# A new order for the 1215 steps of a Mamba-2 and SwiGLU kernel

## The chip, the cores and the metric

The kernel runs on one core of a Trainium2 chip. The metric is the device time of one execution in microseconds (us). Before the change the median of three runs is 358.98 us (358.59 to 359.54). One further execution was taken by the profiler; all rows come from it.

## The reference

```python
def _attn_ref(x, a, B, C):              # x (4, 8, 768, 32), a (4, 8, 768), B and C (4, 8, 768, 16)
    log_a = np.log(np.clip(a, 1e-06, 1.0))
    for c in range(nc):                 # chunks of 32
...
        L = np.exp(cum[:, :, :, None] - cum[:, :, None, :]) * causal
        y_intra = np.einsum('bhij,bhjd->bhid', np.einsum('bhin,bhjn->bhij', Cc, Bc) * L, xc)
        y_inter = np.einsum('bhin,bhnd->bhid', Cc, state) * np.exp(cum)[:, :, :, None]
        y[:, :, sl] = y_intra + y_inter
        state = decay_full[:, :, None, None] * state + np.sum(Bx, axis=2)

def _moe_ref(x, w_gate, w_val, w_out, rms_g):   # x (3072, 256), d_ff 1536
    xn = x / np.sqrt(np.mean(x * x, axis=-1, keepdims=True) + 1e-06) * rms_g
    g = xn @ w_gate
    return (g * (1.0 / (1.0 + np.exp(-g))) * (xn @ w_val)) @ w_out
```

All inputs and the output are fp32. The output y of the first part, with its heads side by side, is the x of the second.

## The kernel before

The 3072 tokens are cut into 12 pairs (256 tokens, p = 0 to 11) for the first part and into 6 blocks (512 tokens, blk = 0 to 5) for the second. The 1536 hidden units are cut into 12 slices of 128 (f = 0 to 11), and the weights are fetched in 18 pieces (k = 0 to 17).

Most products of the second part run in three matmuls of a shorter format (fp32r) in place of one in fp32: an operand is cut into a high part, a low part and a third part, and the three partial products are added in PSUM. For the weights these parts are made on the chip from the fetched bits: `pow` (two ACT operations of L272, `e<-wr,kinks` and `e<-e,kinks`), `mana` (ACT, L306) or `man` (DVE), `wt` (DVE), and then `wH` (ACT, L341), `wHv`, `wL`, `wM`, `wMp`.

The work is written as 1215 steps in one string, `order` (line 1422 on). Each step is a name with numbers, and stands for a function that issues instructions on one engine, or a few. A loop goes through the string and calls them one after the other. Every engine executes its instructions in that order, and buffers are handed out in that order too: six rings, among them the eight banks of PSUM. A step that needs a bank waits until the step that last reads that bank has run. So the string decides what waits for what. Nothing reorders it later.

The steps that the following speaks of:

- `X.blk.f.m` (`gv_split`, L1173): the gate (m = 0) or the value (m = 1) of one slice for one block: six fp32r matmuls with 512 columns. `F` (L1163) and `early` (L1126) are the fp32 forms that the first block uses for a few slices.
- `silu.blk.f` (ACT, L272, `hx<-gv`) and `hid.blk.f` (DVE) turn gate and value into a hidden slice. `hH`, `hL`, `hK` cut it into three parts.
- `OX`, `OY`, `OF` (L1242, L1220, L1248): the product of a hidden slice with the output weights.
- `A.p` (L843), `S.p`, `yi.p` (L929, `y<-T,S`) and `ya.p` (L929, `y<-L,x`): the state sums, the states, and the two parts of y. These matmuls use small tiles of the array: 64x32 for A and ya, 32x64 for yi and for `gb` (L778). `ms` (L1020 and L1027) sums squares, with tiles of 128x32 from block 1 on.
- `yt.blk.k` (ACT, L1005 and L1008): copies two banks of y out of PSUM. `sq` (ACT) squares y, `rs` takes the roots for the norm, `xH`, `xL`, `xK` cut the normed x into its three parts.
- `sums` (L622 and L629), `row`, `turn` (L704), `T`, `Tt`, `L`, `exp`: decays and turned operands of the first part. `i:y.0` and `i:y.1` are the y products of the first two pairs, before early.0.0, the first product of the second part.
- `put`, `puta`, `putva`: the output is copied out of PSUM and stored.

ACT has one set of functions loaded at a time. Exp and silu are in different sets, and where the order of the steps goes from one to the other, a table load (L264 for the silu set, L266 for the exp set) is issued by a helper. A number behind a star in the string (`i:c*2`) asks for that many filler matmuls (L131), whose result is not used, ahead of that step's own.

Of the kernel before, what the change touches and what calls it, by code (L numbers as in the profile page):

```python
# [50 lines left out]
def kernel(  # L51
# [15 lines left out]
    NB, NH, S, D = x.shape  # L67
# [5 lines left out]
    T = NB * S  # L73
# [181 lines left out]
    parts = {}  # L255
# [130 lines left out]
    mid = mids[:, 0]  # L386
# [958 lines left out]
    def token_out():  # L1345
# [77 lines left out]
        i:warm i:a i:set i:bc.0 i:ident i:bc.1 i:bc2.1.1 i:ones i:zeros i:ident16 i:whole i:kinks  # L1423
        i:idle.7 i:after i:never i:fetch.2 i:whole16 i:mean i:part i:head i:part2 i:sel i:after2
        i:mask.0.0 i:upto i:mid i:upto2 i:eps i:aT i:la0 i:log i:mask.0.1 i:mids i:log4.0.4 i:hmask
        p:x.1 i:c*2 p:x.0 i:r.0 i:cx p:turn.0 i:d i:tmask i:gcol i:log4.4.2 i:dx i:log4.6.2
        i:fetch.0 i:parts.0 i:middles p:turn.1 p:Tt.1.0 i:sums.0.1 i:Tb.0 i:mask.1.1 i:cc p:T.0
        i:sums.1.1 i:exp.0.1 i:fetch.6 i:g.0.1 i:exp.1.1 i:sums.0.0 p:scale.1 p:Tt.1.1 i:last.1
        p:scale.0 p:T.1 i:r.1 i:g.0.0 i:exp.0.0 i:L.0.1 i:tok i:Tl.1 i:g.1.1 i:pow.2 i:mask.1.0
        i:parts.1 i:L.0.0 i:last.0 i:sums.1.0 i:A.1 i:exp.1.0 i:row.1 i:A.0 i:L.1.1 i:g.1.0 i:Tl.0  # L1430
        p:S.0 i:tokout p:bc.2 i:pow.0 i:fetch.1 i:y.0 i:rowe.1 p:bc.3 i:sq.0 i:row.0 i:limit i:L.1.0
        i:sums.3 p:S.1 i:man.0 i:pow.6 i:y.1 i:wt.0 i:rowout.1 i:yt.0 p:dT.2 i:fetch.4 p:turn.2
        i:sq.1 i:yt.1 i:early.0.0 i:open i:man.6 i:wt.6 i:man.1 i:fetch.5 i:man.2 i:exp.3 b:ms.0
        i:rowe.0 i:cav.3 i:early.0.1 i:pow.1 i:sums.2 i:wHv.6 i:wt.1 b:rs.0 i:wt.2 i:fetch.3 p:x.2
        p:dT.3 p:x.3 i:fetch.12 i:fetch.8 p:T.2 i:xn i:exp.2 p:Tt.2.1 p:turn.3 p:Td.2 i:early.1.0
        i:norm.0 p:Tt.2.0 p:T.3 p:Tt.3.1 i:wHv.2 i:rowout.0 i:man.4 i:early.1.1 b:F.0.2.0 i:pow.4
        p:scale.3 i:wt.4 p:Tt.3.0 i:norm.1 b:xH.0.1 i:pow.5 i:ca.2 b:gb.1 i:wL.6 b:L.1.1 b:F.0.4.0
        i:fetch.10 p:scalep.2 b:xH.0.0 b:silu.0.2 i:silu.0 b:xLp.0.1 i:pow.3 b:L.1.3 p:Td.3
        b:F.0.3.0 b:L.1.2 b:L.1.0 b:xK.0.1 b:xK.0.0 i:wHv.1 i:mana.3 b:xLp.0.0 p:A.2 p:S.2 p:A.3
        i:wt.3 b:silu.0.4 i:man.5 i:pow.12 b:F.0.5.0 i:wMp.6 b:X.0.7.0 b:X.0.6.0 i:wHv.3 p:S.3  # L1440
        p:qb.5 b:silu.0.5 i:wL.3 b:silu.0.3 i:fetch.9 i:pow.8 i:man.12 i:fetch.11 p:yi.2 i:wt.5
        p:ya.2 i:pow.10 b:silu.0.6 i:wM.3 p:yi.3 p:ya.3 i:fetch.13 i:wHv.5 b:sq.1.0 i:hid.0 i:wt.12
        p:qc.5 i:wL.5 b:X.0.2.1 i:silu.1 b:yt.1.1 i:mana.10 b:hid.0.2 i:gains i:mana.8 p:vB.5
        i:wMp.5 b:silu.0.7 i:wt.10 b:sq.1.1 b:X.0.3.1 i:fetch.7 i:wt.8 i:pow.13 i:man.13 b:yt.1.0
        b:sqav.1 p:spread.8 i:fetch.14 i:hid.1 i:fetch.17 i:pow.11 b:OF.0.0.1 b:X.0.5.1 b:X.0.4.1
        b:ms.1 p:spread.10 b:OF.0.1.1 i:wHv.10 b:OF.0.0.0 i:wt.13 i:wL.10 i:man.11 b:OF.0.2.0
        i:wMp.10 b:rs.1 i:wH.4 i:wH.8 p:qc.4 b:rb.1 b:hid.0.3 b:hid.0.5 i:wt.11 b:OF.0.2.1 i:man.7
        i:wHv.11 i:pow.9 i:man.9 i:wL.11 i:wL.1 p:dT.5 b:OF.0.3.1 i:mana.14 b:X.0.11.0 p:vC.5
        i:pow.7 b:OF.0.1.0 i:wMp.11 p:scale.5 b:hid.0.4 p:spread.11 i:fetch.15 i:wt.9 b:X.0.10.0
        i:man.17 b:OF.0.3.0 i:wL.8 i:wH.9 i:pow.17 i:wL.9 b:silu.0.11 b:X.0.11.1 b:X.0.10.1  # L1450
        b:silu.0.10 i:wM.8 i:wM.9 p:sub.10 p:qb.4 i:wt.17 i:wt.7 i:wH.7 b:X.0.9.1 b:X.0.9.0 p:subp.8
        i:pow.14 p:x.4 i:wH.0 p:vC.4 b:X.0.8.0 b:hid.0.10 p:Tt.5.1 p:spread.9 p:dT.4 p:Tt.5.0
        b:silu.0.8 i:wL.7 b:X.0.8.1 b:OF.0.10.0 i:wM.1 i:wM.7 b:xn.1.1 i:wL.4 p:Tt.4.1 b:X.0.7.1
        b:OF.0.10.1 p:subp.11 b:X.0.6.1 i:wt.14 i:fetch.16 b:OF.0.4.1 i:mana.15 p:scalep.4 b:xn.1.0
        b:hid.0.7 b:OF.0.5.1 b:xH.1.1 b:xK.1.1 b:silu.0.9 p:A.4 p:x.5 p:ex.10 b:xLp.1.1 p:vB.4
        b:xH.1.0 p:ex.8 p:subp.9 b:hid.0.9 p:Tt.4.0 i:pow.15 p:ex.11 b:xL.1.0 b:xK.1.0 p:ex.9
        b:OF.0.4.0 b:X.1.10.0 p:qc.6 p:S.4 i:wH.17 b:hid.0.8 b:X.1.10.1 b:silu.1.10 p:ca.9 p:qc.7
        i:wMp.4 b:hid.0.6 b:X.1.11.0 b:hid.0.11 p:cav.8 p:qb.7 p:A.5 b:hid.1.10 b:X.1.6.0 b:OF.0.5.0
        b:silu.1.11 b:hH.0.7 b:silu.1.6 b:X.1.8.0 b:X.1.8.1 p:Tdp.4 p:scale.6 p:S.5 b:silu.1.8
        i:wL.0 p:ca.11 p:ca.10 i:wt.15 b:hL.0.7 i:wL.17 i:wM.0 b:gb.2 b:hid.1.8 p:vC.7 b:X.1.7.0  # L1460
        i:wH.14 b:L.2.0 b:X.1.11.1 b:silu.1.7 i:mana.16 i:wMp.17 b:L.2.1 p:scalep.7 b:L.2.2 i:wH.15
        b:X.1.0.0 b:L.2.3 i:pow.16 p:Tdp.5 p:vC.6 b:table.2 p:yi.4 i:wL.15 b:silu.1.0 i:wt.16
        i:wM.15 p:x.6 b:hHv.0.11 i:wH.13 p:ya.4 i:wH.16 p:yi.5 p:Tt.7.0 b:hid.1.11 p:ya.5 b:sq.2.0
# [12 lines left out]
        b:OX.1.11.1 b:OX.1.8.1 b:put.0.0 b:hL.1.0 b:OX.1.6.0 b:OX.1.11.0 b:L.3.1 b:xH.2.1 i:wL.13
        b:OX.1.0.1 b:OX.1.6.1 b:L.3.2 b:xLp.2.1 b:xK.2.1 b:L.3.0 b:hH.1.7 p:qc.8 b:L.3.3 b:hHv.1.5
        b:OX.1.0.0 p:Td.7 b:OX.1.8.0 p:qc.11 b:hL.1.7 b:hK.1.7 b:xH.2.0 b:hH.1.1 p:yi.6 p:ya.6
        b:xL.2.0 p:scalep.8 b:xK.2.0 p:yi.7 i:wL.14 p:ya.7 b:hid.1.2 i:wMp.14 p:spread.19 b:OX.1.7.1
        p:vC.8 b:exps.5 p:spread.18 b:yt.3.1 b:sq.3.1 p:qb.10 b:hHv.1.2 b:OX.1.7.0 b:X.2.0.0 p:vB.8  # L1480
        b:X.2.10.0 b:X.2.2.0 b:hHv.1.4 b:hL.1.5 p:spread.16 b:X.2.4.0 b:yt.3.0 p:qc.9 b:hK.1.4
        b:silu.2.10 b:hLp.1.4 b:hK.1.2 p:subp.19 b:hK.1.5 b:hK.1.1 b:X.2.10.1 i:wMp.13 b:silu.2.0
        b:OX.1.4.1 b:OX.1.4.0 b:sq.3.0 p:scale.11 b:X.2.0.1 p:ex.19 b:X.2.7.0 b:hL.1.2 b:silu.2.7
        b:hid.2.0 b:hL.1.1 p:spread.17 b:X.2.9.0 b:OX.1.2.1 b:OX.1.2.0 b:hHv.1.10 b:X.2.11.0 p:vB.10
        p:x.8 b:hLp.1.10 b:hK.1.10 b:OX.1.1.0 b:hH.1.3 p:vC.11 b:OX.1.5.0 p:vB.11 b:silu.2.11
        p:sub.18 b:silu.2.2 p:vC.9 b:sqa.3 b:hHv.1.9 p:Tt.8.0 p:A.8 b:ms.3 p:ca.19 p:sub.16 p:qc.10
        p:S.8 b:OX.1.1.1 p:Tt.8.1 p:sub.17 b:X.2.2.1 b:hL.1.9 b:hLp.1.3 b:OX.1.10.0 b:rs.3
# [101 lines left out]
```

## Time and profile before

| | |
|---|---|
| median of the runs | 358.98 us |
| profiled execution, span | 357.0 us |
| matmuls on PE, in the program | 2394 |
| table loads on ACT | 34 |
| DMA packets, MB | 94556, 27.88 |

The engines in the profile are PE (TensorE matmuls), PEld (its weight loads), DVE (VectorE), ACT (ScalarE), POOL (GpSimd) and SP (which issues DMAs). A timeline row has its start in us, its duration in us, the engine, the line, the operation, output and inputs, the tile of the array, shape and type, and how many like records are put together. An fp32 matmul leaves two records. Matmuls are pipelined, and the ends of their records reach into the next; times of PE are therefore read from start to start. The rows of a stretch give, for each engine, busy us and the number of its instructions, then the granted clock, the share of the DMA engines and GB/s.

### The profile page before, as it was taken

The numbers are of one execution on the slowest core, as the hardware profiler recorded it, in microseconds if no ns is written. First come the engines' busy times: TensorE is split into PE (matmuls) and PEld (weight loads), VectorE is DVE, ScalarE is ACT, GpSimd is POOL, SyncE is SP. The second block draws the span as 40 slices with busy tenths as digits, with TensorE's granted clock in tenths as the row PEclk, the third lists the DMA queues.
The fourth block names the chain that finished last, engine by engine and source line by source line (L and its number), as shares of the span: only waits on it lengthen the run. The fifth ranks groups of instructions, "written<-read, shape, count | busy, mean of one in ns | idle before, by whom it ended". The sixth has DMA issues, their size and how long they took to land.

```text
span 357.0 us, 8314 instructions
## 1 busy us (share of the span) xinstructions
PE 352.7 (99%) x3329; PEld 285.0 (80%) x3329; DVE 283.5 (79%) x507; ACT 196.6 (55%) x338; POOL 91.1 (26%) x91
## 2 busy tenths in 40 slices
PE   8999999999999999999999999999999999999996
PEld 5677578887888878878788788788788888888896
DVE  6899999999998999987887955877357582875791
ACT  3888999994756757494154672463345342112510
POOL 4125314256211326540123320025101111311000
PEclk9999999999999999999999999999999999999999
DMA  8978986672261345443123011200010021001003
GB/s 105 213 124 242 281 233 189 176 162 51 42 155 55 96 81 136 80 76 75 31 64 102 8 31 29 48 14 2 7 31 0 1 37 23 0 0 31 0 2 88
DMA packets 94556, 27.88 MB, mean 78 GB/s; under 512 B 77463, under 2 KB 92471, under 8 KB 94519
## 3 DMA queue, kind: packets, MB, share of 16 engines
q1 hardware_dynamic: 92438, 27.23, 33.4%
q8 instruction: 26, 0.43, 0.5%
q10 hardware_dynamic: 2080, 0.13, 0.4%
q14 instruction: 12, 0.09, 0.1%
HBM read 23.68 MB, written 3.67 MB: 77 GB/s over the span
## 4 chain that ended last, share of the span: by engine, by line
PE 98%; DVE 1%; issue 0%
PE gv L1173 53%; PE o L1242 19%; PE o L1248 8%; PE y L929 3%; PE o L1220 2%; PE gv L1163 2%; PE gv L1126 2%; PE g L778 2%; PE A L843 1%; PE g L771 1%; PE e L608 1%; PE y L904 1%; PE e L622 1%; PE ms L1027 0%; PE idle L447 0%; PE row L1311 0%
## 5 line engine op out<-in xcount | busy, mean ns | idle before, releaser
L1173 PE MATMUL gv<-xh,wh 128*128 128x512 f32 x272 | 87.0, 401 | 0.0
L272 ACT ACTIVATE hx<-gv 128x512 f32<-128x512 f32 x70 | 40.2, 595 | 80.2 <-PE gv L1173 36.7
L1173 PE MATMUL gv<-xl,wp 128*128 128x512 f32 x272 | 84.1, 390 | 0.0
L1173 PE MATMUL gv<-xk,wp 128*128 128x512 f32 x272 | 83.8, 390 | 0.0
L1096 DVE SCALAR_TENSOR_TENSOR hk<-hx,hh 128x512 fp32r<-128x512 f32 x65 | 53.0, 827 | 25.4 <-PE o L1242 18.9
L1094 POOL TENSOR_TENSOR hl<-hx,hh 128x512 fp32r<-128x512 f32 x21 | 29.7, 1418 | 131.1 <-DVE hk L1096 30.4
L1173 PEld LDWEIGHTS gv<-xl,wp 128*128 128x128 f32 x272 | 51.1, 188 | 11.0
L1173 PEld LDWEIGHTS gv<-xk,wp 128*128 128x128 f32 x272 | 51.1, 188 | 10.9
L1173 PEld LDWEIGHTS gv<-xh,wh 128*128 128x128 f32 x272 | 50.0, 188 | 10.8 <-issue 0.6
L1188 DVE SCALAR_TENSOR_TENSOR hx<-gv,hx 128x512 f32<-128x512 f32 x70 | 47.0, 684 | 13.4 <-PE gv L1173 12.4
L341 ACT ACTIVATE hh<-hx 128x512 fp32r<-128x512 f32 x37 | 22.8, 629 | 39.8 <-PE o L1242 11.9
L1242 PE MATMUL o<-hh,wh 128*128 128x512 f32 x96 | 37.9, 395 | 0.0
L1242 PE MATMUL o<-hl,wp 128*128 128x512 f32 x96 | 37.4, 390 | 0.0
L1242 PE MATMUL o<-hk,wp 128*128 128x512 f32 x96 | 37.4, 390 | 0.0
L1094 DVE TENSOR_TENSOR hl<-hx,hh 128x512 fp32r<-128x512 f32 x44 | 31.1, 721 | 2.8 <-PE o L1242 1.3
L266 ACT ACT_TABLE_LOAD x17 | 21.8, 1283 | 1.1 <-PEq L1573 0.8
L264 ACT ACT_TABLE_LOAD x17 | 21.8, 1283 | 0.3
L1242 PEld LDWEIGHTS o<-hh,wh 128*128 128x128 f32 x96 | 18.0, 188 | 4.2 <-issue 0.4
L336 POOL TENSOR_TENSOR wp<-wh,wp 128x512 fp32r<-128x512 f32 x9 | 13.0, 1449 | 32.6 <-DVE wp L328 25.0
L1242 PEld LDWEIGHTS o<-hk,wp 128*128 128x128 f32 x96 | 18.0, 188 | 3.8
L1242 PEld LDWEIGHTS o<-hl,wp 128*128 128x128 f32 x96 | 18.0, 188 | 3.6
L328 DVE SCALAR_TENSOR_TENSOR wp<-wh,w 128x512 fp32r<-128x512 f32 x27 | 19.6, 751 | 0.0
(184 smaller groups left out, 548.2 us busy)
## 6 DMA issues: line engine op xcount, KB each, us to landing
L<-rowd SPq DMA_DIRECT2D x32, 128.0 KB
x<-in_x_dram SPq DMA_DIRECT2D x24, 128.0 KB
wr<-in_moe_w_out_dram SPq DMA_DIRECT2D x6, 511.5 KB
wr<-in_moe_w_gate_dram SPq DMA_DIRECT2D x5, 511.5 KB
wr<-in_moe_w_val_dram SPq DMA_DIRECT2D x5, 511.5 KB
out_dram<-ob SPq DMA_DIRECT2D x28, 64.0 KB
bc<-in_B_dram SPq DMA_DIRECT2D x23, 64.0 KB
bc<-in_C_dram SPq DMA_DIRECT2D x23, 64.0 KB
```

The source lines that it names most:

```text
L264: nc.scalar.preload_act_table(AF.Silu)
L266: nc.scalar.preload_act_table_set("natural_log_exp_and_others")
L272: nc.scalar.activation(**operands)
L328: nc.vector.scalar_tensor_tensor(out=(low_parts, mixed_parts)[i][k], in0=high_parts[k], scalar=(-UP, GAIN)[i], in1=view(ws[k], shape), op0 ...
L336: nc.gpsimd.tensor_tensor(out=mixed_parts[k], in0=high_parts[k], in1=low_parts[k], op=ALU.subtract)
L341: nc.scalar.activation(out=out, in_=in_, func=AF.Copy, scale=scale)
L1094: engine.tensor_tensor(out=out, in0=v, in1=high, op=ALU.subtract)
L1096: nc.vector.scalar_tensor_tensor(out=out, in0=v, scalar=REST, in1=high, op0=ALU.mult, op1=ALU.subtract)
L1173: nc.tensor.matmul(out=o, lhsT=weights_of(m, t, f)[part], rhs=view(x, [P, TB], F32R), start=(part == t == 0), stop=(part == 2 and t == 1))
L1188: nc.vector.scalar_tensor_tensor(out=v, in0=o, scalar=gain(blk, f), in1=v, op0=ALU.mult, op1=ALU.mult)
L1242: nc.tensor.matmul(out=o, lhsT=w[:, b * P:(b + 1) * P], rhs=v, start=opens, stop=True, skip_group_check=True)
L1248: nc.tensor.matmul(out=o[:, j * DM:(j + 1) * DM], lhsT=v[:, tk], rhs=w, start=opens, stop=True, skip_group_check=True)
```

## The change

The string is replaced by another order of the same 1215 steps. The multiset of the steps is the same but for one: `i:c*2` becomes `i:c`, so the two filler matmuls are gone (2392 matmuls in the program). The number of operations of all other kinds stays, except for the table loads, which the order of exp and silu decides: 38 in place of 34. Nothing else changes; the lines behind the string move by six.

```diff
@@ -1420,134 +1420,140 @@
     order = """
...
-        p:x.1 i:c*2 p:x.0 i:r.0 i:cx p:turn.0 i:d i:tmask i:gcol i:log4.4.2 i:dx i:log4.6.2
...
+        i:r.0 i:log i:c i:upto2 i:fetch.0 i:middles i:sel p:x.1 p:turn.0 i:tmask i:cx i:gcol
...
```

Three places show what moves. The first is PE at the y products of block 1, pairs 2 and 3. `y<-T,S` is yi, `y<-L,x` is ya, `gv` is an X step, `o<-w,hx` an OF step; xN counts like instructions in a row. Before:

```order
L1173 MATMUL gv<-xk,wp 128x512 x2
L929 MATMUL y<-T,S 64x64 x16
L929 MATMUL y<-L,x 32x64 x32
L929 MATMUL y<-T,S 64x64 x12
L929 MATMUL y<-L,x 32x64 x32
L1173 MATMUL gv<-xh,wh_822 128x512 x2
```

And now:

```order
L1173 MATMUL gv<-xk,wp 128x512 x2
L929 MATMUL y<-L,x 32x64 x64
L929 MATMUL y<-T,S 64x64 x28
L1248 MATMUL o<-w,hx 128x256 x8
L1027 MATMUL ms<-sq,mean 32x128 x4
L1173 MATMUL gv<-xh,wh_891 128x512 x2
```

The two yi and the two ya stand together, which leaves one change of tile between them in place of three; four OF steps and the sums of squares of block 1 follow at once. The y products of the other blocks are put together in the same way.

The second place is ACT from the squares of block 1 to the second copy of its y. `sq<-y` is sq, `hx<-gv` and `u<-u` silu, `w<-wr,kinks` mana, `wh` wH, the pairs of `e<-` pow, and the two rows of `yt<-y` are yt.1.1 and then yt.1.0. Before:

```order
L272 ACTIVATE sq<-y 128x4x64 x2
L272 ACTIVATE u<-u 128x512
L1005 COPY yt<-y 128x4x64
L1008 COPY yt<-y 64x4x64 x2
L306 ACTIVATE w<-wr,kinks 128x512 x2
L272 ACTIVATE hx<-gv 128x512
L272 ACTIVATE sq<-y 128x4x64 x2
L272 ACTIVATE e<-wr,kinks 128x512
L272 ACTIVATE e<-e,kinks 128x512
L1005 COPY yt<-y 128x4x64
L1008 COPY yt<-y 64x4x64 x2
```

And now:

```order
L272 ACTIVATE sq<-y 128x4x64 x4
L306 ACTIVATE w<-wr,kinks 128x512
L1005 COPY yt<-y 128x4x64
L1008 COPY yt<-y 64x4x64 x2
L341 ACTIVATE wh_999<-w 128x512
L272 ACTIVATE hx<-gv 128x512
L272 ACTIVATE e<-wr,kinks 128x512
L272 ACTIVATE e<-e,kinks 128x512
L272 ACTIVATE e<-wr,kinks 128x512
L272 ACTIVATE e<-e,kinks 128x512
L341 ACTIVATE wh_1041<-w 128x512
L1005 COPY yt<-y 128x4x64
```

Between the two copies now stand two pow and two wH in place of two mana, the squares and one pow. On PE, three X steps (X.0.3.1, X.0.8.0, X.0.9.0) follow the sums of squares, and X.0.2.1 behind them is given the bank that the second copy empties.

The third place is ACT around the first hidden slices of block 1. `L<-L` is the exponential of the decays (`ex`), `hx<-gv` silu. Before:

```order
L266 ACT_TABLE_LOAD
L272 ACTIVATE L<-L 128x512
L341 ACTIVATE xh<-yt 128x512
L272 ACTIVATE L<-L 128x512
L341 ACTIVATE T<-T,tmask 128x256
L272 ACTIVATE e<-wr,kinks 128x512
L272 ACTIVATE e<-e,kinks 128x512
L272 ACTIVATE L<-L 128x512 x2
L341 ACTIVATE wh_1343<-w 128x512
L264 ACT_TABLE_LOAD
L272 ACTIVATE hx<-gv 128x512 x2
```

And now, with silu.1.11 between two of the exponentials and silu.1.10 first behind them:

```order
L272 ACTIVATE L<-L 128x512
L264 ACT_TABLE_LOAD
L272 ACTIVATE hx<-gv 128x512
L266 ACT_TABLE_LOAD
L272 ACTIVATE L<-L 128x512 x2
L341 ACTIVATE T<-T,tmask 128x256
L264 ACT_TABLE_LOAD
L272 ACTIVATE hx<-gv 128x512 x4
```

One silu has moved in among the exponentials, and each side of it has a table load.

More of the change, by code (lines that the diff above doesn't have):

```diff
@@ L1428 @@
[L1428 to L1463, printed above, removed]
```

224 lines of the change are left out of this document (133 added, 91 removed).

## The prediction

> **What bounds the kernel now.** I read the page's busy shares and its chain first, then the wait view, then the stretches of the span, then the timelines of TensorE (PE) and ScalarE (ACT).
>
> ```profile
> span 357.0 us, 8314 instructions
> PE 352.7 (99%) x3329; PEld 285.0 (80%) x3329; DVE 283.5 (79%) x507; ACT 196.6 (55%) x338; POOL 91.1 (26%) x91
> PE 98%; DVE 1%; issue 0%
> PE idle L447 <- DVE warm L489: 1.1, 1, 1.1
> ```
>
> The span is 357.0 us, PE is busy for 99% of it, the chain that ends last is PE for 98%, and the wait view (last row) knows one wait of PE in the whole run: 1.1 us at the start. So only three things can move the time: how long PE's own stream takes, a wait that is new in it, or the stretch before its first matmul and behind its last. The last matmul starts at 353.64 and the span ends 3.4 us later, with the copy and the store of the last output:
>
> ```profile
> 353.64 0.28 PE L1220 MATMUL o<-wp,hk 128*128 128x256 f32 x1
> ```
>
> How near the others are to making PE wait differs by stage:
>
> ```profile
> core 0: us, PE busy (x) PEld busy (x) DVE busy (x) ACT busy (x) POOL busy (x), PEclk, DMA share, GB/s
> 41.00:72.00 31.00, 31.00 (x316) 25.16 (x315) 30.82 (x59) 29.52 (x53) 8.01 (x6) 1.00 0.75 205
> 126.00:357.00 231.00, 227.92 (x1866) 188.96 (x1853) 165.03 (x262) 99.61 (x163) 48.79 (x39) 1.00 0.18 38
> ```
>
> Between 41 and 72 us ACT is busy 29.5 of 31.0 us and VectorE (DVE) 30.8. Nobody has slack there; a step that comes some us earlier in PE's order than its operand in ACT's becomes a wait. Behind 126 us ACT is busy for 99.6 of 231 us and DVE for 165.0, so the new order is free there to put PE's work as it likes. The granted clock is 1.00 throughout.
>
> **What PE's stream gains.** The multiset of steps is the same, so almost every matmul keeps its duration. What an order can change is how often PE goes from one shape of tile to another. Pair products as they stand now, two A products alone and side by side, and one row of weight loads:
>
> ```profile
> 93.59 0.49 PE L929 MATMUL y<-T,S 32*64 32x64 f32 x32
> 94.00 0.86 PE L929 MATMUL y<-L,x 64*32 64x64 f32 x64
> 94.79 0.49 PE L929 MATMUL y<-T,S 32*64 32x64 f32 x32
> ...
> 77.01 0.45 PE L843 MATMUL A<-x,Bd 64*32 64x64 f32 x32
> 77.39 0.48 PE L1248 MATMUL o<-w,hx 128*128 128x256 f32 x1
> ...
> 107.67 0.86 PE L843 MATMUL A<-x,Bd 64*32 64x64 f32 x64
> 108.45 0.74 PE L1173 MATMUL gv<-xh,wh 128*128 128x512 f32 x2
> ...
> 94.00 0.70 PEld L929 LDWEIGHTS y<-L,x 64*32 64x32 f32 x64
> ```
>
> From start to start, yi takes 0.41 us and ya 0.79. The order now makes yi, ya, yi, ya of two pairs; the change makes yi, yi, ya, ya (or ya, ya, yi, yi): two changes between small shapes fewer for each of five blocks. With the sums, A and g products counted too, I find 20 changes between small shapes before and 9 after: 11 fewer. Their price isn't in any row by itself. Low end: a stretch of 64 records of one shape (two A, 107.67 to 108.45) takes 0.78, no less than twice the stretch of 32 (77.01 to 77.39: 0.38, so 0.76); merging then brings 0. High end: in such a stretch 64 weight loads take 0.70 of 0.79 us, so 0.09 is left over at a change, and about 0.14 if the next operands load meanwhile. I take 0.09: 11 x 0.09 = **1.0 us** gained, between 0 and 1.5. One small stretch fewer between large products (15 instead of 16) saves a change in and a change out, at 0.09 to 0.14 each some 0.25. Together **1.3 us**. The two filler matmuls (L131) that go belong to the head.
>
> **The head, up to the first split product.** Until 22.8 us the end is set by a chain over PE, ACT and DVE, after it by PE alone.
>
> ```profile
> 23.28 1.89 PE L1126 MATMUL gv<-yt,w 128*128 128x256 f32 x8
> ...
> 27.68 0.44 PE L622 MATMUL e<-row,sel 32*64 32x64 bf16 x32
> ...
> 28.27 0.66 PE L704 MATMUL tp<-ident,bc 128*128 128x128 f32 x4
> ...
> 40.94 1.03 PE L1173 MATMUL gv<-xh,wh 128*128 128x512 f32 x2
> 41.81 0.62 PE L1173 MATMUL gv<-xl,wp 128*128 128x512 f32 x2
> 42.27 0.62 PE L1173 MATMUL gv<-xk,wp 128*128 128x512 f32 x2
> ...
> 53.56 2.64 PE L1248 MATMUL o<-w,hx 128*128 128x256 f32 x11
> ```
>
> The first output products come about 1.3 us earlier in the new order, but sums.2 (27.68 to 28.27: 0.59), sums.3, the two row sums and turn.2 are put between them and early.0.0, which so starts near 23.6 instead of 23.28. Since sums.2 is no longer behind it, that is a gain of 0.2 at most. Then F.0.5.0 waits for weight piece 4 at about 32.4, as late as it comes now. I take the first X at 41.0 as in 40.94: **0**, +-0.5. Two weights of PE's first microseconds:
>
> ```profile
> 2.76 1.01 PE L608 MATMUL e<-whole,ident 128*128 128x512 bf16 x2
> 9.30 0.60 PE L608 MATMUL e<-whole,ident 128*128 128x512 bf16 x2
> ```
>
> The same mask products take 1.01 at 2.76 us and 0.60 at 9.30. By the Trainium skill ("TensorE: Matmul & The Clock Gate", Part 1) PE runs at half rate until it has been busy for about 3.4 us, so taking fillers away speaks against the change; by that rule the four early masks could cost up to 0.8 us more, but the granted clock in the rows here reads 1.00 and these products wait for nothing in the chain that ends at 22.8, so the sum stays.
>
> **The wait that ACT adds.** In the new order, X.0.2.1 takes the bank that the first copy of yt.1.0 empties, and ACT has much ahead of that copy. The durations, from start to start:
>
> ```profile
> 26.07 0.69 ACT L272 ACTIVATE r<-ms,eps 128x512 f32<-128x512 f32 x1
> ...
> 33.13 0.62 ACT L341 ACTIVATE xh<-xn 128x512 fp32r<-128x512 f32 x1
> 33.65 0.77 ACT L272 ACTIVATE e<-wr,kinks 128x512 f32<-128x512 int16 x1
> 34.45 0.72 ACT L272 ACTIVATE e<-e,kinks 128x512 int16<-128x512 f32 x1
> 35.08 0.61 ACT L341 ACTIVATE xh<-xn 128x512 fp32r<-128x512 f32 x1
> 35.71 1.28 ACT L264 ACT_TABLE_LOAD   x1
> 37.00 0.60 ACT L272 ACTIVATE hx<-gv 128x512 f32<-128x512 f32 x1
> ...
> 47.58 0.37 ACT L1005 COPY yt<-y 128x256 f32<-128x256 f32 x1
> ...
> 48.74 1.43 ACT L306 ACTIVATE w<-wr,kinks 128x512 f32<-128x512 uint32 x2
> 50.06 0.60 ACT L272 ACTIVATE hx<-gv 128x512 f32<-128x512 f32 x1
> 50.53 0.66 ACT L272 ACTIVATE sq<-y 128x256 f32<-128x256 f32 x2
> 51.06 0.78 ACT L272 ACTIVATE e<-wr,kinks 128x512 f32<-128x512 int16 x1
> ...
> 52.51 0.36 ACT L1005 COPY yt<-y 128x256 f32<-128x256 f32 x1
> ```
>
> From rs.0 to the copy the new order has: rs.0 1.25 (two operations like the 0.69 at 26.07); eight pow at 1.43 (33.65 to 35.08), 11.4; six high parts at 0.53, 3.2; four turned tiles and one row of decays at about 0.4 (the like of the copy at 47.58: 0.37 of 128x256), 2.1; one table load 1.29; eight silu at 0.5, 4.0; three mana at 0.66, 2.0; two sq at 0.53, 1.1; yt.1.1 1.16. Sum 27.5, and some 0.5 of waits in between. The same sum over the order of before gives 26.6; measured is 52.51 - 26.07 = 26.44. rs.0 comes 0.5 later in the new order (the early steps are behind sums.2): 26.6 + 27.5 + 0.5 = 54.6, with the copy's 0.36 it is 55.0. PE is there earlier: from 41.0 five X of three pairs at 0.46 (41.81 to 42.27), 6.9, with 0.4 lost behind F (40.94 to 41.81 is 0.87), the y products of two pairs 2.2, four OF at 0.86 (2.64 for 11 of three steps' 12 records), 3.4, ms 0.4 and the changes around them 0.3, is 54.6. So PE waits **0.4 us**, between 0 and 2. Behind the waiting X.0.2.1 stands all the rest of PE's work, so it counts in full. The second place is ACT between 71 and 88 us:
>
> ```profile
> 72.94 1.28 ACT L266 ACT_TABLE_LOAD   x1
> ...
> 79.29 1.28 ACT L264 ACT_TABLE_LOAD   x1
> ```
>
> Here are two loads; the new order has four (38 in all instead of 34), 2 x 1.28 = 2.6 us more for ACT, and X.1.6.1 needs the bank of silu.1.10. Counted on from the copy by the same durations, ACT ends that at about 86.2 and PE is there at 88.4: 2.2 us to spare, so 0. By the Trainium skill ("ScalarE: Activation LUTs", What ACT_TABLE_LOAD costs) a switch costs a drain of 1.38 us beside the load's 1.28; by that rule four loads would take 5.5 us more and PE would wait 3.3 there, which makes 361.5. The trace has no room for it: the load at 35.71 starts when the operation before it ends (35.08 + 0.61), and the next one starts 1.29 later. Behind 126 us no step of the new order stands nearer to its operand than DVE's and ACT's lead allows, but for the last hK, which reaches OX.5.11.0 some 0.1 ahead; the last steps (OY products, one copy by ACT, one by DVE) are the same two kinds, so the 3.4 us behind the last matmul stay.
>
> **Sum.** 357.0 + 0 - 1.3 + 0.4 = 356.1 for the span. The median of the runs is 358.98, the span 357.0, so 2.0 lie around it; the profiled execution is taken as a median one. **358.2 us** (0.8 below 358.98). About 0.3%, or 1.08 us, is what a measurement can tell from no change: faster means below 357.9, slower above 360.06.
>
> **The rivals.**
> *The wait doesn't come.* If ACT is at the copy 0.5 sooner (as in 26.07 for rs.0), 0.4 of wait falls away, and if a change between shapes is worth its high end, 0.5 more is gained: 358.2 - 0.9 = 357.3, with bounds of 356.5 (a head 0.5 to 0.8 shorter too) and 357.8 (the wait alone). For it: ACT's rows leave ends 0.06 to 0.1 inside the next, so its pace is as good as I took it. Against it: the eight pow ahead of yt.1.0.
> *Merging brings nothing.* The A rows (0.78 for twice 0.38) are the nearest, and by them 1.0 of gain falls away: 359.2, no change.
> *ACT becomes the bound between 41 and 88 us.* With whole durations instead of start to start (pow 0.06 and silu 0.1 longer) eight of each make X.0.2.1 wait 1.3 more. ACT then slips on at the same rate over the next 31 us, 1.4 more, and with 0.6 for the waits of the two further loads it goes past the 2.2 us to spare at X.1.6.1; from there each 0.1 of slip is a 0.1 of PE. A slip of 3.3 costs 1.1 there: 358.2 + 1.3 + 1.1 = 360.6, slower. For it: ACT's 29.5 of 31.0 us. Against it: it holds today with the same operations.
> *The reordering doesn't reach the engines* isn't open: each executes its part of the list in order.
>
> **How the numbers follow.** Forecast 358.2, own range 357.4 to 359.0: 0.42 (faster 0.13, same 0.29). No wait: 0.28 (faster 0.26, same 0.02). Merging brings nothing: 0.12 (same 0.10, slower 0.02). ACT the bound: 0.18 (slower 0.16, same 0.02). Faster 0.39, same 0.43, slower 0.18. The range, 356.6 to 360.7, leaves out the lower end of the first rival and what ACT could lose beyond its price.
>
> **What would show it.** In the profile of the changed kernel: the first X near 41.0; a wait of PE for yt's copy (L1005) of about 0.4 us near 54.6 and none at silu near 88; y products as two stretches a block with one change, together 2.2 instead of 2.4; ACT loads x19 and x19; the last matmul near 352.7 with 3.4 behind it. The prediction is wrong if PE shows waits of over 1 us anywhere, or if the merged y stretches take as long as the four of before.

## The result, and the profile after

The changed kernel takes 372.63 us (median of 4 runs, 371.34 to 373.53) against 358.83 before (median of 4): 1.0376 times as long, with a 95% interval of 1.0351 to 1.0401. That is 13.8 us slower, far outside the range that was given.

From the page of the changed kernel, its busy shares, table loads and the chain that ended last:

```profile
span 371.8 us, 8293 instructions
...
PE 355.8 (96%) x3327; PEld 285.0 (77%) x3327; DVE 286.9 (77%) x507; ACT 202.7 (55%) x342; POOL 93.8 (25%) x91
...
PE 63%; DVE 21%; SPq 8%; issue 5%; DMA 3%; ACT 0%; POOL 0%; DVEq 0%
...
L266 ACT ACT_TABLE_LOAD x19 | 24.4, 1283 | 2.2 <-issue 1.9
L264 ACT ACT_TABLE_LOAD x19 | 24.4, 1283 | 0.3
```

PE, which carried 98% of the chain, now carries 63%, and DVE 21%. PE's idle time is 371.8 - 355.8 = 16.0 us, where it was 4.3: 11.7 of the 14.8 us that the span has grown. The other 3.1 is more busy time of PE. A part of it stands right behind the waits: a row of eight `early` records takes 1.99 us behind the wait of 1.4 us, and 1.89 without a wait.

Whom PE waits for, in the wait view of the changed kernel (us in total, times, longest; `...` stands for rows left out, among them the 1.4 us at the start):

```profile
PE g L778 <- DVE T L193: 1.5, 1, 1.5
PE gv L1126 <- DVE w L312: 1.4, 1, 1.4
...
PE gv L1173 <- DVE xk L1096: 1.3, 2, 1.0
PE gv L1163 <- DVE w L312: 1.3, 1, 1.3
PE y L929 <- DVE L L801: 1.1, 3, 0.6
PE gv L1173 <- DVE wp L328: 1.0, 1, 1.0
PE o L1242 <- POOL hl L1094: 0.9, 1, 0.9
...
PE gv L1173 <- ACT hx L272: 0.2, 1, 0.2
```

Nearly every row has DVE's name, in many different steps. ACT, which the prediction followed, is there once, with 0.2 us. The waits begin at early.1.0, the third of the `early` products, and end by 146 us, but for the 0.9 us for POOL, which come at 255.7. In the stretch from 22.8 to 110 us DVE is as busy as before (85.60 us of 87.20, against 85.45), but it gets through less: 143 operations in place of 160. The first row is of the kernel before, the second of the changed one; behind the stretch and its length come PE, PEld and then DVE, each with its busy time and its count:

```profile
22.80:110.00 87.20, 87.20 (x1067) 67.96 (x1064) 85.45 (x160) 72.46 (x131) 32.46 (x29) 1.00 0.65 162
```

```profile
22.80:110.00 87.20, 78.42 (x911) 58.92 (x910) 85.60 (x143) 66.83 (x113) 35.49 (x29) 1.00 0.62 152
```

So DVE's single operations have become slower. Where it begins can be seen in DVE's timeline of the changed kernel, with POOL's for the same time behind it:

```profile
24.02 0.73 DVE L312 SCALAR_TENSOR_TENSOR w<-w,e 128x512 int16<-128x512 int16 x1
...
26.67 1.36 DVE L300 TENSOR_SCALAR w<-wr 128x512 f32<-128x512 uint32 x1
...
28.15 1.46 DVE L312 SCALAR_TENSOR_TENSOR w<-w,e 128x512 int16<-128x512 int16 x1
...
31.99 0.68 DVE L1139 TENSOR_TENSOR u<-gv,r 128x512 f32<-128x512 f32 x1
32.59 0.67 DVE L1139 TENSOR_TENSOR hx<-gv,r 128x512 f32<-128x512 f32 x1
33.19 0.41 DVE L300 TENSOR_SCALAR w<-wr 128x512 f32<-128x512 uint32 x1
33.71 1.63 DVE L312 SCALAR_TENSOR_TENSOR w<-w,e 128x512 int16<-128x512 int16 x1
```

```profile
25.57 3.46 POOL L644 TENSOR_SCALAR_AFFINE_SELECT L<-L 64x1024 f32<-64x1024 f32 x2 [0.25 <-ACT L L272]
...
31.88 2.86 POOL L1094 TENSOR_TENSOR xl<-xn,xh 128x512 fp32r<-128x512 f32 x2 [1.82 <-ACT xh L341]
```

The same operation (L312, `wt`) takes 0.73 us at 24.02, started with POOL idle, and 1.46 and 1.63 while POOL runs; `man` (L300) takes 0.41 or 1.36. The two long `wt` end 0.58 and 0.61 us after the POOL operation that they met, the long `man` 0.28: each 0.12 to 0.15 us less than it takes alone. So they wait for POOL's operation to end, and then do their work. This holds over the whole of both traces: the stretched operations with two 128x512 fp32 operands, 0.65 to 0.68 us alone, end 0.54 to 0.55 us after POOL's, whether they lose 0.2 us or 1.1, and those that take 0.41 alone end 0.27 to 0.29 after it. One `man`, at 33.19, takes its 0.41 although POOL runs: it started within 0.02 us of POOL's operation. The two L1139 rows run beside POOL without losing anything; they read PSUM (`gv`). In the order of before, the same mask on POOL stands elsewhere (POOL's timeline of the kernel before):

```profile
29.54 2.64 POOL L644 TENSOR_SCALAR_AFFINE_SELECT L<-L 64x1024 f32<-64x1024 f32 x2 [5.12 <-ACT L L272]
```

There DVE had begun xn (L1070) before it, and then ran L747 and L1139, which read PSUM. Only one operation, the following `wHv` of 1.04 us, was held up.

Over both traces, these are the DVE operations that find a POOL operation running when they start, with at least 0.2 us of it to come (from 20 us on). The first number of each pair is how many of them are stretched, which means over 0.15 us longer than the shortest tenth of the same line and shape in the two traces:

```
                                          before           after
one operand or the result in PSUM         0 of 39          0 of 26
transposes L193, SBUF to SBUF, one input  0 of 8           0 of 3
all others, operands in SBUF only         42 of 46         44 of 46
```

The Trainium skill ("SBUF — State Buffer", Who interferes with whom) says that VectorE's second pair of SBUF ports is GpSimd's only pair, and that an operation of VectorE with two SBUF inputs (against one of GpSimd that reads SBUF), or in a mode that uses both ports, and one of GpSimd exclude one another for their whole length, while one with a single SBUF input outside such a mode does not contend. The first two rows of the table agree with that, and the third does where there are two inputs; `man` and `wHv`, which have a single SBUF input and are held up too, agree if they run in such a mode, which no record shows. It is the rule that bore on this change, and my prediction didn't use it.

In all, these operations lose 27 us before and 31 after, and what matters is where. Between 22.8 and 110 us, where DVE is busy 98% of the time, the operations of before lose 7.0 us, 12 of them over 0.25 us each; those of the changed order lose 15.7 us, 23 of them over 0.25 us. Where the experiments below speak of the stretch "up to 110 us", this sum is meant.

### The profile page after: what moved, and what is told of

It is laid out like the page before. It is cut to its first block, busy times and chain, and to the rows that moved or that the text cites. A ratio compares the mean times of both kernels' runs of the same rounds, so it can differ in the third digit from the quotient of the medians.

```text
span 371.8 us, 8293 instructions
## 1 busy us (share of the span) xinstructions
PE 355.8 (96%) x3327; PEld 285.0 (77%) x3327; DVE 286.9 (77%) x507; ACT 202.7 (55%) x342; POOL 93.8 (25%) x91
## 4 chain that ended last, share of the span: by engine, by line
PE 63%; DVE 21%; SPq 8%; issue 5%; DMA 3%; ACT 0%; POOL 0%; DVEq 0%
PE gv L1173 37%; PE o L1242 16%; PE o L1248 3%; SPq L160 3%; DVE wp L328 2%; PE o L1220 2%; DVE hx L1188 2%; DVE w L312 2%; DVE w L300 2%; PE gv L1163 2%; DVE hk L1096 1%; DVE L L801 1%; DVE S L872 1%; SPq L173 1%; PE g L778 1%
## 5 line engine op out<-in xcount | busy, mean ns | idle before, releaser
L1173 PE MATMUL gv<-xh,wh 128*128 128x512 f32 x272 | 85.6, 396 | 1.2 <-DVE hk L1096 0.7
L1094 POOL TENSOR_TENSOR hl<-hx,hh 128x512 fp32r<-128x512 f32 x21 | 30.8, 1475 | 127.3 <-PE o L1242 52.4
L1096 DVE SCALAR_TENSOR_TENSOR hk<-hx,hh 128x512 fp32r<-128x512 f32 x65 | 51.2, 800 | 14.2 <-PE o L1242 12.0
L341 ACT ACTIVATE hh<-hx 128x512 fp32r<-128x512 f32 x37 | 22.7, 627 | 35.2 <-PE o L1242 9.7
L1094 DVE TENSOR_TENSOR hl<-hx,hh 128x512 fp32r<-128x512 f32 x44 | 33.5, 768 | 9.8 <-PE o L1242 5.1
L336 POOL TENSOR_TENSOR wp<-wh,wp 128x512 fp32r<-128x512 f32 x9 | 14.2, 1584 | 37.8 <-DMA wr<-in_moe_w_val_dram 20.2
L644 POOL TENSOR_SCALAR_AFFINE_SELECT L<-L 64x512 f32<-64x512 f32 (+1 forms) x18 | 16.0, 887 | 21.2 <-DMA r<-roots 9.9
```

The costliest lines, as they stand in the source:

```text
L336: nc.gpsimd.tensor_tensor(out=mixed_parts[k], in0=high_parts[k], in1=low_parts[k], op=ALU.subtract)
L341: nc.scalar.activation(out=out, in_=in_, func=AF.Copy, scale=scale)
L644: nc.gpsimd.affine_select(out=L[r], in_=L[r], pattern=[[0, L.shape[1]], [1, HC]], compare_op=ALU.is_ge, fill=0.0, base=0, channel_multipli ...
L1094: engine.tensor_tensor(out=out, in0=v, in1=high, op=ALU.subtract)
L1096: nc.vector.scalar_tensor_tensor(out=out, in0=v, scalar=REST, in1=high, op0=ALU.mult, op1=ALU.subtract)
L1173: nc.tensor.matmul(out=o, lhsT=weights_of(m, t, f)[part], rhs=view(x, [P, TB], F32R), start=(part == t == 0), stop=(part == 2 and t == 1))
```

## The experiments

Two theories stood against one another. *Collision*: the new order puts DVE's SBUF-only operations on top of POOL's, and DVE, which has no slack up to 110 us, comes too late for PE. *List*: DVE's new list has work ahead of urgent steps, whatever POOL does. A third was added later: *late results*, PE and DVE wait for what POOL makes. In the labels, a is the changed kernel, b the one before. A kernel that leaves work out gives another result; only its time is used.

### One mask on POOL left out (a_no_ca2)

```diff
-        p:turn.3 i:ca.2 i:wL.6 p:T.3
+        p:turn.3 i:wL.6 p:T.3
```

> The changed kernel without one step: the causal mask of pair 2 on POOL (ca.2, 3.4 us on POOL from 25.57 on) is left out and nothing takes its place. Theory 1, collision (a DVE operation that touches only SBUF and finds POOL running waits until POOL's operation ends): man.1 (1.36 us) and wt.1 (1.46 us) go back to 0.41 and 0.73, early.1.0 no longer waits for wt.1 (1.44 us in the changed kernel), and the first split product comes 1.4 to 2.9 us earlier than 43.95; the time falls by 1 to 2.9 us. Theory 2, list (DVE simply has too much work ahead of the urgent steps, whatever POOL does): DVE's list is the same, so the wait and the time stay within 0.5 us.

Measured: 371.47 us (369.93 to 372.53). The median is 1.2 below the changed kernel's, within what collision gave, though the ranges of the runs overlap by a little. The clock hides a part: PE's granted clock was 0.994 and 0.995 over three of the four runs (at half speed from 106.4 to 109.9 us in the profiled one) and 1.00 in the fourth, which took 369.93 us, 2.7 less than the changed kernel, whose runs were all at 1.00. DVE's timeline is clearer than the time:

```profile
26.91 0.41 DVE L300 TENSOR_SCALAR w<-wr 128x512 f32<-128x512 uint32 x1
...
27.44 0.73 DVE L312 SCALAR_TENSOR_TENSOR w<-w,e 128x512 int16<-128x512 int16 x1
...
32.24 1.63 DVE L312 SCALAR_TENSOR_TENSOR w<-w,e 128x512 int16<-128x512 int16 x1
```

Both operations are back at 0.41 and 0.73, and PE's first wait for `wt` fell from 1.4 to 0.2 us. The first split product starts at 42.47 instead of 43.95. The next `wt` (32.24) still runs into a POOL operation (xLp) and PE's second wait, 1.3 us, stays.

### Eight POOL steps in place left out (a_no_inplace)

```diff
-        i:ca.2  p:subp.8 p:subp.9 p:subp.11  p:ca.9 p:ca.10 p:ca.11 p:ca.12
```

> The changed kernel without eight POOL steps that work in place on the decays (the masks ca.2, ca.9, ca.10, ca.11, ca.12 and the subtractions subp.8, subp.9, subp.11): left out, nothing in their place. By the collision theory the DVE operations that ran beside them in the changed kernel lose 6.5 us of their stretch (man.1 0.96, wt.1 0.73, wt.14 0.84, man.17 0.85, xK.1.1 0.85, S.5 0.75, hK.0.11 and hL.0.11 0.99, hHv.0.6 0.33, Td.7 0.25), PE's waits for DVE fall by 4 to 6.5 us and the time comes to 366 to 369 us. By the list theory it stays at 372 to 373 us.

Measured: 366.82 us (366.44 to 368.58), 5.8 us less than the changed kernel, within what collision gave. DVE's list is unchanged, so list alone can't have made that. But the time is still 7.9 us above before, with little more stretch up to 110 us than before has (9.9 us, 14 operations over 0.25 us). So either the list was the other half, or the stretches that were left sat at places where PE waits.

### Eleven POOL steps done by DVE (a_pool_to_dve)

```diff
-   i:ca.2 p:scalep.4 i:wMp.5 i:wMp.10 i:wMp.11 i:wMp.4 i:wMp.12 p:subp.8 p:subp.9 p:subp.11 b:xLp.1.1
+   i:cav.2 p:scale.4 i:wM.5 i:wM.10 i:wM.11 i:wM.4 i:wM.12 p:sub.8 p:sub.9 p:sub.11 b:xL.1.1
```

> The changed kernel with eleven POOL steps of the first 90 us done by DVE at the same places of the order (ca.2, scalep.4, wMp.5, wMp.10, wMp.11, wMp.4, wMp.12, subp.8, subp.9, subp.11, xLp.1.1). This gives DVE 7.7 us of operations more (1.21 + 0.41 + 5 x 0.67 + 3 x 0.68 + 0.69) and takes POOL's away. By the collision theory 8.9 us of stretch go (man.1 0.96, wt.1 0.73, wHv.10 0.94, wL.7 0.44, man.11 0.76, wL.9 0.28, man.13 1.11, wt.14 0.84, man.17 0.85, xK.1.0 1.10, xK.1.1 0.85), so DVE is at the end of the stretch about 1 us earlier: the time is 370 to 373 us. By the list theory, with no price on a collision, DVE is 7.7 us later and the time is 378 to 381 us.

Measured: 375.92 us (374.69 to 377.89), between the two expectations: 3.3 slower than the changed kernel. The stretch up to 110 us did fall, from 15.7 to 7.6 us, but 7.7 us of operations came in for it. The rest has a cause that neither theory had. PE waited up to 2.4 us at one place, and its clock fell to half speed at two, for 3.4 us each time (35.2 to 38.7 and 89.9 to 93.3). Stretches of this run, whose bounds reach a little beyond the slow time (the third figure from the end is the granted clock) and two pairs of rows of PE's timeline:

```profile
35.00:38.60 3.60, 3.52 (x4) 1.03 (x4) 3.43 (x11) 0.89 (x1) 0.00 (x0) 0.53 1.01 359
38.60:42.00 3.40, 3.40 (x70) 2.03 (x70) 3.40 (x7) 3.20 (x6) 0.00 (x0) 0.99 0.57 206
...
89.30:93.00 3.70, 3.67 (x10) 2.88 (x11) 3.63 (x10) 2.38 (x3) 0.00 (x0) 0.58 0.52 79
93.00:97.00 4.00, 4.00 (x19) 3.28 (x18) 4.00 (x5) 3.42 (x6) 3.65 (x4) 0.97 0.18 53
```

```profile
89.33 0.50 PE L1173 MATMUL gv<-xl,wp 128*128 128x512 f32 x1 [2.42 <-DVE xl L1094]
...
91.20 1.05 PE L1173 MATMUL gv<-xl,wp 128*128 128x512 f32 x2
92.06 1.05 PE L1173 MATMUL gv<-xk,wp 128*128 128x512 f32 x2
...
94.01 0.63 PE L1173 MATMUL gv<-xk,wp 128*128 128x512 f32 x2
94.47 0.61 PE L1173 MATMUL gv<-xh,wh 128*128 128x512 f32 x2
```

Two matmuls take 0.86 us from start to start (91.20 to 92.06) in the slow time, and 0.46 later (94.01 to 94.47). The granted clock of the four runs was 0.991, 0.982, 0.986 and 0.986 over their whole length. If every lost cycle cost its time, 370 to 371 us would be left, within what collision gave; that is an estimate, and the most that the clock can have cost. List, at 378 to 381, lies above every run even with the lost clock in it. The run also shows that work taken from POOL is no gain if a full DVE gets it.

### The y products merged in the kernel before (b_merged_y)

```diff
-        p:yi.2 ... p:ya.2 ... p:yi.3 p:ya.3
+        p:yi.2 ... p:yi.3 p:ya.2 p:ya.3
...
```

> The kernel before with one part of the change alone: the first ya of each of five blocks is put behind the second yi, so that yi, yi, ya, ya stand together (ten changes between small tiles fewer). The prediction's price is 0.09 us each: 0.9 us faster, 358.0. By the changed kernel's rows (128 records of ya 1.59 us, 56 of yi 0.86) a merged block takes 2.45 us against 2.38 of the four stretches before: no gain, 358.8 to 359.3.

Measured: 359.54 us against 358.97, ratio 1.0013 (1.0002 to 1.0023): no gain, if anything a loss of 0.6. Its profile has PE waiting for DVE by 1.0 us in sum, which it doesn't in the kernel before, so the time alone could hide a small gain. PE's busy time doesn't: it is 352.7 us on the page of either kernel. The merged stretches of the changed kernel say the same (PE's timeline):

```profile
47.19 1.65 PE L929 MATMUL y<-L,x 64*32 64x64 f32 x128
48.78 0.94 PE L929 MATMUL y<-T,S 32*64 32x64 f32 x56
49.64 3.72 PE L1248 MATMUL o<-w,hx 128*128 128x256 f32 x16
```

128 records of ya take 1.59 us and 56 of yi 0.86; the two ya and two yi stretches of before took 2 x 0.79 and 0.41 + 0.39. Nothing is saved by the changes of tile that went.

### POOL's work cut off, in both kernels (a_narrow_pool, b_narrow_pool)

```diff
-            nc.gpsimd.affine_select(out=L[r], in_=L[r], pattern=[[0, L.shape[1]], [1, HC]],
+            nc.gpsimd.affine_select(out=L[r, 0:1], in_=L[r, 0:1], pattern=[[0, 1], [1, HC]],
...
-        nc.gpsimd.tensor_tensor(out=mixed_parts[k], in0=high_parts[k], in1=low_parts[k],
-                                op=ALU.subtract)
+        mixed_parts[k] = low_parts[k]
...
+        if engine is nc.gpsimd:
+            hl[blk, f] = b = hh[blk, f]
...
```

> The changed kernel with nearly no work on POOL behind the head: masks, subtractions and products in place cover one head (or 16 or 32 columns) only, and the third weight parts and low parts that POOL would make are left out (an operand that is there already is read in their place). DVE's, ACT's and PE's lists stay as they are. If the collisions are all of the loss, the stretch of 20.9 us in 28 DVE operations between 22.8 and 150 us goes to under 3, PE's waits go, and the time is 357 to 360 us. If the order of DVE's own list is the other half (the kernel without eight POOL steps still took 366.8 with as little stretch as before the change), PE still waits about 7 us: 364 to 367 us.

> Control: the kernel before with the same cut to POOL's work. PE waits for nothing in it, so DVE gains up to 14.8 us of stretch that no one uses: 357.5 to 359.5 us by either theory.

Measured: 359.37 us for the changed order (ratio to the kernel before 1.0015, 1.0003 to 1.0027) and 359.07 for the order of before (1.0004, 0.9995 to 1.0014). POOL is busy for 23.0 us in place of 93.8 in the changed order, and 13.3 of the 13.8 us are gone, with DVE's, ACT's and PE's lists as the change made them. The list theory (364 to 367) falls. What is left in the wait view of a_narrow_pool, whose lines stand some places lower:

```profile
PE idle L446 <- DVE warm L488: 1.4, 1, 1.4
PE gv L1182 <- DVE hk L1105: 0.8, 1, 0.8
PE gv L1172 <- DVE w L312: 0.5, 1, 0.5
...
```

The mean of L300 between 22.8 and 110 us tells the same (DVE's groups by line in that window; the figure behind the comma is the mean in ns), first of the changed kernel, then of this one:

```profile
L300 DVE TENSOR_SCALAR w<-wr 128x512 f32<-128x512 uint32 x11 | 8.2, 747 | 0.0
...
L1188 DVE SCALAR_TENSOR_TENSOR hx<-gv,hx 128x512 f32<-128x512 f32 x13 | 8.7, 676 | 0.0
```

```profile
L300 DVE TENSOR_SCALAR w<-wr 128x512 f32<-128x512 uint32 x10 | 4.2, 422 | 0.0
...
L1197 DVE SCALAR_TENSOR_TENSOR hx<-gv,hx 128x512 f32<-128x512 f32 x17 | 11.4, 682 | 1.2 <-PE gv L1182 1.2
```

`man`, which only touches SBUF, goes from 747 to 422 ns; `hid`, which reads PSUM, stays at 676 and 682. But this kernel also takes away every wait for a result of POOL's. The next one puts the work back without the results.

### POOL's work done, but for nobody (a_shadow_pool)

```diff
-        ("h", 512, 22), ("q", 1024, 5), ("k", 256, 5), ("s", 64, 9), ("d", 2048, 1))]
+        ("h", 512, 21), ("q", 1024, 5), ("k", 256, 5), ("s", 64, 9), ("d", 2048, 1))]
...
-        nc.gpsimd.tensor_tensor(out=mixed_parts[k], in0=high_parts[k], in1=low_parts[k],
-                                op=ALU.subtract)
+        nc.gpsimd.tensor_tensor(out=spare_r.rearrange("p (k f) -> p k f", k=shape[1]),
+                                in0=high_parts[k], in1=low_parts[k], op=ALU.subtract)
+        mixed_parts[k] = low_parts[k]
+
+    spare = const.tile([P, 512], FP32, name="spare")
...
```

The first pair of lines takes one buffer of 22 from a ring, `h`.

> The changed kernel with POOL's work behind the head done in full and at its places, but into a spare tile that nobody reads (the masks, the differences of products and of decays, the low and third parts are left out of the result; an operand that is there already is read in their place). With the same work cut off, the time was 359.4, which leaves two readings: DVE is held up by POOL's running (collision), or PE and DVE wait for what POOL makes and get it late. If it is the collision, the loss comes back although nothing of POOL's is read: 368 to 373 us, with 15 us or more of stretch in DVE between 22.8 and 150 us. If it is POOL's late results, the time stays at 358.5 to 361 us.

Measured: 375.16 us (373.66 to 376.88). The loss is back although almost nothing that POOL makes behind the head is used (five `scalep` products, 4.8 us, and a sum of squares still are, as they were in a_narrow_pool); collision gave 368 to 373, and the time is above that. The stretch up to 110 us is 14.4 us in 23 operations, as in the changed kernel (15.7 in 23), and in a_narrow_pool 1.5 in 3. PE's waits are DVE's again:

```profile
PE gv L1186 <- DVE w L312: 2.4, 1, 2.4
PE gv L1196 <- DVE wp L328: 1.9, 1, 1.9
PE o L1272 <- DVE L L817: 1.8, 2, 1.6
...
PE gv L1196 <- DVE hx L1211: 1.0, 2, 0.8
PE gv L1149 <- DVE w L312: 0.9, 1, 0.9
```

So late results are not what costs. A buffer that POOL still reads can still be waited for in this kernel: DVE waits twice for POOL's operations into the spare tile, 1.2 and 0.6 us. What the kernel takes beyond 373 wasn't tried apart, but the clock is a part of it: PE ran at half speed from 75.1 to 78.5 and from 139.9 to 143.4 us in the profiled run, and the granted clock of the four runs was 0.991, 0.986, 0.995 and 0.995. With all lost cycles taken off, 370 to 373 us are left, an estimate of the least that the kernel would take at full clock.

### Copies on POOL that nobody reads, in the kernel before (b_pool_early, b_pool_late)

```diff
+    def copied_by_pool(k):
+        for t in range(high_parts[k].shape[1]):
+            for c in range(0, high_parts[k].shape[2], P):
+                nc.gpsimd.tensor_copy(out=spare, in_=high_parts[k][:, t, c:c + P])
...
-        i:wHv.6 i:wt.1 ...
+        i:wHv.6 i:pool.6 i:wt.1 ...
```

> The kernel before, whose order stays, with 18 times some 1.3 us of copies on POOL that nobody reads, each started when a weight's high part is ready (27 to 120 us). No DVE operation is added. By the collision theory DVE's SBUF operations beside them are stretched, by 0.4 to 0.9 us each, 6 to 14 us in all, and PE, which waits for nothing now, waits for DVE: 363 to 371 us. By the list theory (what matters is DVE's own list) 358.5 to 360 us.

> Control: the same 18 copies in the kernel before, put between 195 and 270 us, where DVE is busy for two thirds of the time. DVE's operations are stretched there as well, but its lead over PE takes it up: 358.5 to 360 us by either theory.

Measured: 373.00 us (370.32 to 374.34) early and 358.90 late (ratio 1.0001, 0.9992 to 1.0011). The late copies cost nothing, as expected. The early ones cost 14 us, but not in the way expected, and that run tells nothing for the collision. The wait view of b_pool_early:

```profile
PE gv L1180 <- POOL wp L336: 4.9, 2, 4.2
PE gv L1180 <- POOL xl L1101: 2.9, 1, 2.9
PE y L936 <- POOL T L750: 1.5, 1, 1.5
...
```

PE waits for POOL itself: the 72 copies and DVE held one another up until POOL was busy for 60 of 87 us between 22.8 and 110, and its own steps came late. DVE's stretch was 10.0 us. PE's waits of 2.9 and 4.2 us were each followed by 3.4 us at half clock, so a part of the 14 us is the clock here too.

### POOL's operations cut in pieces (a_split_pool2, a_split_pool4)

```diff
-            engine.tensor_tensor(out=out, in0=v, in1=high, op=ALU.subtract)
+            w = TB // 2 if engine is nc.gpsimd else TB
+            for c in range(0, TB, w):
+                engine.tensor_tensor(out=out[:, c:c + w], in0=v[:, c:c + w], in1=high[:, c:c + w],
+                                     op=ALU.subtract)
...
```

> The changed kernel with POOL's masks, subtractions, low and third parts done in two halves each; the result is the same. By the collision theory a DVE operation waits for the end of the POOL operation that runs, which is now half as long: its mean stretch falls from 0.75 to some 0.4 us, unless DVE then meets the second half too. POOL itself pays a second fixed cost. 366 to 371 us. If the length of a POOL operation doesn't matter, 372 to 374 us.

> The same in four quarters. By the collision theory the stretch falls to 0.2 us a piece: 363 to 370 us, unless POOL, which is then held up by DVE between its pieces, becomes late itself (its operations of 1.3 us would take 2 to 3): then 372 us or more, with PE waiting for POOL by name.

Measured: 369.73 us in halves (369.0 to 370.31) and 371.71 in quarters (371.09 to 372.27). Halves give back 2.9 of the 13.8 us. In quarters the stretch up to 110 us falls further (13.8 us in halves, 9.2 in quarters), but POOL is then busy for 141.2 us in place of 93.8 (111.6 in halves) and PE waits for it by name, 1.7 us for `wp` alone. Shorter operations move waits from DVE to POOL. Whether quarters are worse than halves stays open: the halves ran at a clock of 1.00, the quarters at 0.991 to 0.995, and with the lost cycles taken off the quarters would be at 369 to 370 us (an estimate), where the halves are.

### One mask moved forward in the kernel before (b_ca2_early)

```diff
-        i:sums.3 ... i:yt.0 p:dT.2 ... i:exp.3 b:ms.0 ... i:pow.1 i:sums.2 ... i:xn i:exp.2
+        i:sums.3 ... i:yt.0 i:sums.2 p:dT.2 ... i:exp.3 i:exp.2 b:ms.0 ... i:pow.1 ... i:xn
```

> The kernel before with one pair of steps moved: sums.2 and exp.2 go ahead of early.0.0 and ms.0, as the new order has them, so that the causal mask of pair 2 on POOL (ca.2, 2.6 us) starts at about 25.6 instead of 29.54. DVE's own list stays. In the kernel before ca.2 runs beside xn (already begun), Td.2 and norm.0, which it doesn't hold up (one stretch of 0.63); moved, it meets man.2 or cav.3, wHv.6, wt.1 and wt.2, which only touch SBUF. By the collision theory 1.5 to 2.5 us of stretch appear on DVE between 25 and 30 us, PE waits 0.8 us or more for wt.1 at early.1.0 or for the next weights, and the time is 359.7 to 361.5 us. If the place of POOL's operation doesn't matter, 358.5 to 359.3 us.

Measured: 360.23 us (360.14 to 360.98) against 358.87, ratio 1.0036 (1.0022 to 1.0050): 1.4 us slower, as collision gave. POOL's mask now starts at 26.38, and on DVE:

```profile
26.18 1.70 DVE L300 TENSOR_SCALAR w<-wr 128x512 f32<-128x512 uint32 x2
27.80 2.15 DVE L659 TENSOR_TENSOR L<-L,limit 128x1024 f32<-128x1024 f32 x1
```

Two `man` took 0.74 together and cav.3 (L659) 1.21 in the kernel before. That is 1.9 us of stretch. DVE comes to these steps 0.8 us later than in the kernel before (the first `man` of this row at 24.91 instead of 24.12), but that alone wouldn't make PE wait: without the stretch `wt.1` would end near 29.0, and PE is ready for it at 29.87. With the stretch PE waits 1.1 us, with the same line in its wait view that the changed kernel has:

```profile
PE gv L1126 <- DVE w L312: 1.1, 1, 1.1
```

One mask at another time makes the first wait of the new order in the old one.

## Why the prediction was wrong

**What bounds the kernel.** This was right for the kernel before, and the prediction even read that DVE has no slack between 41 and 72 us (30.8 of 31.0). The step that failed comes right behind it: of the two engines without slack, only ACT was followed to a wait. DVE's operations were never put into a sum. Their durations were taken to be what they are in the old order, but those of the SBUF-only ones depend on what POOL does at that moment, and the order decides that. The sum had no term for it; it measured 8.7 us more of stretch up to 110 us (15.7 against 7.0) and some 9 us of PE's waits for DVE. Behind 126 us, where the new order was taken to be free, PE waits 1.6 us at three places. Both signs of being wrong that the prediction named came: waits of over 1 us, and merged stretches that take as long as the four of before.

**The head**, taken as 0 +-0.5, is the first term that this broke: the first split product starts at 43.95 instead of 40.94, 3.0 us late, by two waits for `wt` of 1.4 and 1.3 us. early.0.0 itself starts at 23.55, as the prediction had it (23.6). The argument that weight piece 4 "comes as late as it comes now" was wrong: its `wt` was one of the stretched operations (1.63). The clock of 1.00 that the prediction read for the first microseconds is no reading: the trace's record of the clock begins 5.0 us into the span of the kernel before, and a row without a record prints 1.00.

**The wait that ACT adds**, 0.4 us at X.0.2.1, is not in the trace; PE was later there than ACT (the copy ends at 57.3 us, X.0.2.1 starts at 57.9). The second place, X.1.6.1, waits 0.24 us for silu. The four loads around it cost nothing more.

**Merging**, 1.0 us gained, was worth nothing for the y products, as the rival had it whose price came from the A rows. The counts were right: the traces have 20 changes between small shapes behind the first split product before and 9 after, and 16 and 15 small stretches. The price was wrong: it took the leftover of the weight loads for a gain. The merged stretches show that a longer stretch takes as much more; why wasn't tried by itself.

**The rival on the other side** had the right kind of event, an engine that becomes the bound between 41 and 88 us, but named ACT, gave it 0.18, and so ended at 360.6.

**The sum without POOL** can be judged from the two kernels with POOL cut off: 359.37 and 359.07. Apart from the collisions, the new order is worth nothing that can be told from zero, where the prediction had 0.8 us of gain. The two profiles show a gain inside that: with the new order PE is busy for 350.5 us instead of 352.7, and the first split product starts at 40.28 instead of 40.95. But PE waits 0.8 and 0.5 us for DVE, which it doesn't in the order of before, and is idle for 2 us more in all. From the first split product to the last matmul, its waits left out, PE takes 312.0 us instead of 312.6: a gain of 0.6 where the prediction had 1.3. Each of these is one execution, and what in the order makes the 0.6 wasn't tried apart. The same order takes 5.3 us more of PE's busy time with POOL's work in it (355.8), so the waits cost PE more than their length.

That the collisions are the cause rests on four runs together: the loss goes when POOL is cut off and not the lists (a_narrow_pool), comes back with work whose results are hardly used (a_shadow_pool), shrinks when single POOL steps are left out (a_no_inplace) and can be put into the old order by moving one mask (b_ca2_early). How much of the 13.8 us is DVE's stretch and how much the direct waits for POOL (0.9 and 0.6 us at two places in the changed kernel) or waits for buffers or the longer matmuls behind a wait wasn't separated further.

## What to carry to other kernels

Before an order is judged by sums of durations, ask for each engine whether its durations hold in the new order: here VectorE's operations on SBUF cost 0.4 or 1.4 us depending on whether GpSimd was running, and an order that looked equal by the old durations lost 3.8%. Where VectorE is full, GpSimd's work belongs into a stretch where VectorE has slack (18 times four copies late in the program cost nothing), or beside VectorE's PSUM reads, none of which was held up (0 of 65), though no run here tried to place it so. A search over a timetable needs that exclusion in its model; moving the work to VectorE or cutting it in pieces gave back little or made it worse.

## What the runs showed of the hardware that was not expected

PE's granted clock fell to 0.50 for 3.4 us at a time, behind waits that were mostly shorter than that. It did so eight times in these profiles: at 106.4 us in a_no_ca2, 103.8 in a_split_pool4, 35.2 and 89.9 in a_pool_to_dve, 75.1 and 139.9 in a_shadow_pool, 47.1 and 74.4 in b_pool_early. In the 3.4 us ahead of each fall PE was busy for 0.15 to 0.67 of the time. Only one of the waits there was longer than 3.4 us (4.2, b_pool_early). The length of a wait alone doesn't decide: one of 2.4 us in a_shadow_pool (36.05), and two of 1.8 us, in a_pool_to_dve (65.9) and a_split_pool2 (34.2), were followed by full speed, as were all waits of the changed kernel, up to 1.5 us. Within a run, falls and recoveries lie whole multiples of 3.41 us apart in the trace's record (a_shadow_pool: 75.08, 78.50, 139.94 and 143.35), so where a wait lies to that beat may decide; no run tried it. The Trainium skill ("TensorE: Matmul & The Clock Gate", Part 1) has PE fall to half speed after an idle window of about 3.4 us that runs freely. The speed and the 3.4 us agree, but PE was not idle for all of such a time in seven of the eight cases. Each fall can cost up to 1.7 us on top of the wait, half of its 3.4 us (an estimate).
